# An attention and Fourier kernel on one core: 18 of 64 chunks of scores computed twice instead of 20, in the order of a restated plan

## The chip, the core and the metric

The kernel runs on one core of one Trainium2 chip. The time is the device time of one execution in microseconds; lower is better. A core has five engines that work side by side: TensorE (PE, matmuls; PEld is its loading of weights), VectorE (DVE), ScalarE (ACT), GpSimd (POOL), and SyncE (SP), which here issues every DMA. Each works through its own list of instructions in order and waits on semaphores for the others.

## What is computed

Two independent parts, both in float32, with sequence length S = 2048 and width D = 448. Their results stand side by side in the output (2048 x 896).

```python
# A: Fourier mixing, real part
a = x @ dft_hid_re.T;  b = x @ dft_hid_im.T          # 2048 x 448 each
y = dft_seq_re @ a - dft_seq_im @ b                  # 2048 x 2048 times 2048 x 448, twice
# B: softmax attention, H = 16 heads of Dh = 28
q, k, v = heads(x @ wqkv)
p = softmax(q @ k.T * Dh ** -0.5)                    # 2048 x 2048 for each head
out_b = (p @ v) @ wo
```

## The kernel before

**Products.** Float32 accuracy comes from splitting each operand into a high part (rounded to the fast matmul type fp32r) and a low part (the rest, by a subtraction), and adding three products: high x high, high x low, low x high. ACT rounds a piece (`whi`, L516), POOL subtracts (`wlo`, L522). All of part A, the projections of part B and the output projection are made of such matmuls with 448 or 512 columns: L547 for projections, values and the hidden Fourier step, L662 for the Fourier step along the sequence, L987 for the output projection.

**Attention.** A *unit* is a head h and a chunk c of 512 queries; there are 16 x 4 = 64. For a unit the scores against all 2048 keys are made in 16 matmuls of 128 x 512. The softmax subtracts a maximum first, and there are two ways to get at it:

- `unit_twice`: 16 score matmuls with the queries on the partitions (L754), each followed by a maximum over the row on DVE (L758). The row maxima (`nm`, L762) are turned by a small matmul (L717), split in two parts (L766, L767), written to a scratch tensor in HBM (`nmd`, L773) and read back as two more rows of the operand `q` (L775). Then 16 score matmuls again, now with the keys on the partitions and the maximum already subtracted (L786), and 16 exponentials on ACT straight from PSUM (L790).
- `unit_kept`: 16 score matmuls with the keys on the partitions (L808). ACT copies the scores to SBUF (L415), DVE keeps a running maximum over the 16 tiles (`rm`, L815 and L818). The maximum over partitions is made on DVE with a transpose (L823), reductions (L825, L835), small copies between partitions (L830, L833) and a transpose back (L841); ACT copies it to SBUF (`mb`, L843). Then the maximum is added (negated) to the kept scores, two tiles at a time, on POOL or on DVE (both L858), and ACT takes 8 exponentials over pairs (L862).

For both kinds PE then multiplies by the values, in two groups of 8 matmuls (`pv_group`, L735), and the result is copied out (`ou`). When a head is done, or at the end a chunk of the last two heads, `out_of` adds up four partial sums (L877), fetches the softmax's denominators through a small DMA (`sm`, L882), inverts them, writes them out (`rd`, L884), reads them back spread over partitions (L888), multiplies on POOL (L891) and stores to `ond` (L894). At the very end the output projection reads `ond` (L951, L956), splits it (L969 and L411) and multiplies (L987).

`TWICE` says which chunks of which head are computed twice.

**Order of work.** The order of every engine's list is worked out when the kernel is built. Work is added as tasks with an engine, an assumed duration, a key (when it is due) and what it depends on; `Schedule.run` then plays a clock forward, and whenever an engine is free in that play it takes the ready task with the lowest key and emits its instructions. Keys of units come from two lanes, the twice units and the kept ones, each spread evenly from `T_ATT` to `T_END`; the keys of the Fourier and projection matmuls (`fkey`) run up to `T_FILL`, those of the output projection from `T_OUT`. The assumed durations are constants such as `RAW` (what a DVE instruction adds when it needs the result of the one before), `SMALL` (a small DVE step), `PE_TURN` (PE changes its tile shape), `M448` and `MS` (matmuls). On the chip the engines wait on semaphores, so an assumed duration that is off changes the order and the waits, not the result.

A task ends three times in the play: its engine is free, its result may be used by the same engine ("own"), and its result is seen by the others ("seen"). A DMA's engine is SP, which is free after the issue, long before the data has landed.

Of the kernel before, what the change touches and what calls it, by code (L numbers as in the profile page):

```python
# [14 lines left out]
ALU = mybir.AluOpType  # L15
AX = mybir.AxisListType
# [22 lines left out]
N_WARM = 11  # L39
GV = 8  # L40

TWICE = [(1, 3) if h in (2, 5, 9, 12) else (1,) for h in range(H - 2)] + [(3,), (3,)]
OUT_DVE = True

LAST = (0, 1, 3, 2)
# [8 lines left out]

RAW = 0.16
LANES = 8
FLOW, FLOW_IN = 200.0, 400.0
T_IN = 20.0  # L60
# [1 line left out]
FLOW_AT = 4.1  # L62
X_ROWS = 2.0
AHEAD = 0.15
PE_TURN = 0.22


class Slot:
# [101 lines left out]
class Schedule:  # L170
# [34 lines left out]
    def run(self):  # L205
# [10 lines left out]
        while True:  # L216
            for e in self.ENGINES:
                if not idle[e]:
                    continue
                aside, pick, first = [], None, None  # L220
                if e == "SP" and len(landed) >= LANES and landed[-LANES] > now + 1e-9:
                    heapq.heappush(events, (landed[-LANES], 2, count, "tick", None))
                    continue
                heap = self.ready[e]
                before = now - (AHEAD if e == "PE" else 0.0) + 1e-9
                while heap:
                    item = heapq.heappop(heap)
                    t = item[2]
                    if t.n in done:
                        continue  # L230
                    wants = {}
                    for s in t.use:
                        if s.i is None:
                            wants.setdefault(s.pool, []).append(s)
                    if t.since > before or any(not p.can_take(w, before, now) for p, w in wants.items()) or any(
                            x.lock > now + 1e-9 for x in t.lock):
                        aside.append(item)
                        continue
                    if e == "PE" and mode == 1 and t.mode == 0 and pick is None:
                        if not any(x[2].mode == 1 and x[2].n not in done for x in heap):  # L240
                            pick = t
                            break
                        first = first or item
                        aside.append(item)
                        continue
                    pick = t
                    break
                if pick is None and first:
                    pick = first[2]
                    aside.remove(first)  # L250
                for item in aside:
                    heapq.heappush(heap, item)
                if pick is None:
                    continue
                t = pick
                done.add(t.n)
                for s in t.use:
                    if s.i is None:
                        s.pool.take(s)
                dur = t.engs[e]  # L260
                if e == "PE":
                    if t.mode > mode:
                        dur += PE_TURN
                    mode = t.mode
                lat = t.lat
                if e == "SP":

                    at = now
                    for size, extra in t.dmas:
                        if len(landed) >= LANES:  # L270
                            at = max(at, landed[-LANES])
                        flow = max(flow, at + 0.4) + size / (FLOW if now > T_IN else FLOW_IN)
                        landed.append(max(at + 1.35 + size / 170 + extra, flow + 1.1))
                        at += 0.38
                    dur = at - now
# [14 lines left out]
            while events and events[0][0] <= now + 1e-9:  # L290
# [2 lines left out]
                    idle[x[0]] = True  # L293
                elif what == "own":
                    for n in x[1].then:
                        if x[0] in n.engs and len(n.engs) == 1:
                            n.left -= 1
                            if n.left == 0:
                                self.wake(n)
                elif what == "seen":  # L300
# [3 lines left out]
                        if s.users == 0:  # L304
                            s.home.free.append((s.i, now))
                    for n in t.then:
                        if e in n.engs and len(n.engs) == 1:
                            continue
                        n.left -= 1
                        if n.left == 0:  # L310
                            self.wake(n, now)
# [6 lines left out]
def tile_kernel(ctx, tc, xa, wre, wim, wd, xb, wqkv, wo, out):  # L318
# [67 lines left out]
    eng = {"ACT": nc.scalar, "DVE": nc.vector, "POOL": nc.gpsimd}  # L386


    M512, M448, MS = 0.2335, 0.2065, 0.2365
    ACT_P, ACT_S, DVE_P, POOL_2, SMALL = 0.48, 0.52, 0.60, 1.25, 0.11  # L390

    def pe(key, emit, n=1, d=MS, lat=0.25, **kw):
        return sch.add({"PE": n * d}, key, emit, lat=lat, **kw)
# [8 lines left out]
    def dve(key, emit, d=DVE_P, **kw):  # L402
        return sch.add({"DVE": d}, key, lambda e: emit(), **kw)
# [391 lines left out]
    def unit_kept(u):  # L795
# [6 lines left out]
        for kt in range(NT):  # L802
# [17 lines left out]
        key = t_a + 16 * dt - 20  # L820

        o = bank_s.slot()
        t = dve(key, lambda o=o: nc.vector.transpose(o.t, rm.t), 0.64, deps=[prev], acq=[o], use=[rm])  # L823
        pm = bank_s.slot()
        r = dve(key, lambda o=o: nc.vector.tensor_reduce(  # L825
            pm.t[:, :NT], o.t.rearrange("p (j r) -> p j r", r=32), axis=AX.X, op=ALU.max, negate=True), deps=[t], use=[o, pm], own=RAW)
# [8 lines left out]
        r = dve(key, lambda o=o: nc.vector.tensor_reduce(  # L835
            o.t[:32, :NT], pm.t[:32, :4 * NT].rearrange("p (i j) -> p j i", i=4), axis=AX.X, op=ALU.min), 0.17,
            deps=r, use=[pm, o], own=RAW)
        for n in (32, 64):
            r = dve(key, back(n), SMALL, deps=[r], use=[o], own=RAW)

        t = dve(key, lambda o=o: nc.vector.transpose(pm.t, o.t[:, :NT].unsqueeze(2).to_broadcast([P, NT, 32])), 0.64,  # L841
                deps=[r], use=[pm, o], own=RAW)
        ld = act(key, lambda: nc.scalar.activation(mb.t, pm.t, AF.Copy), deps=[t], use=[pm, mb], lock=[pm])  # L843
        po = bank_s.slot()
        last_pv = None
# [187 lines left out]
```

## Time and profile before

| | |
|---|---|
| median of 3 runs | 1165.56 us (1164.64 to 1166.68) |
| profiled execution, own time | 1163.75 us |
| its span, first to last instruction | 1161.9 us |
| mean granted TensorE clock | 0.999 |
| busy: PE, DVE, ACT, POOL | 1145.3, 1010.8, 1029.1, 884.6 us |
| DMA | 125.19 MB, 35.8% of the 16 DMA engines |

The busy time of an engine is the time in which at least one of its instructions runs. Matmuls follow each other into PE before the one ahead has ended, so the duration of one is longer than what it adds to PE's list; what it adds is seen from start to start. Waits are put down to the instruction that released the waiting one last. A row of the groups reads: line, engine, operation, tiles written <- tiles read, shape, count | busy us, mean ns of one | idle time of the engine just before them, and what ended most of it.

### The profile page before, as it was taken

How to read it: one execution, taken by the hardware profiler on the slowest of the kernel's cores; microseconds unless marked ns; L12 is line 12 of the kernel's file. 1: busy time of each engine (PE TensorE's matmuls, PEld its weight loads, DVE VectorE, ACT ScalarE, POOL GpSimd, SP SyncE). 2: the span in 40 equal slices, each digit the busy share in tenths (PEclk: the TensorE clock that was granted, in tenths of full speed). 3: DMA queues.
4: the chain of work that ended last, by engine and by line, in shares of the span. 5: the costliest groups of instructions: out<-in, count | busy, mean ns of one | idle time of the engine just before them, and what ended most of it. 6: DMA issues, size and time to landing. Idle time of an engine off the chain costs nothing.

```text
span 1161.9 us, 19485 instructions
## 1 busy us (share of the span) xinstructions
PE 1145.3 (99%) x6110; PEld 778.7 (67%) x6110; DVE 1010.8 (87%) x1803; ACT 1029.1 (89%) x1748; POOL 884.6 (76%) x521
## 2 busy tenths in 40 slices
PE   8999999999999999999999999999999999999998
PEld 7876556656676667767666656566666667766677
DVE  6599989999898989999899999998989998799832
ACT  5269999999999899999899999999999999899952
POOL 2138687888789888978888897987989899596630
PEclk9999999999999999999999999999999999999999
DMA  8893344222223222232333232232423223323543
GB/s 259 176 214 120 125 140 148 66 83 73 82 85 102 85 85 82 73 114 78 89 105 100 86 96 65 85 101 90 120 80 96 88 87 114 120 73 92 162 158 109
DMA packets 111880, 125.19 MB, mean 108 GB/s; under 512 B 49368, under 2 KB 63352, under 8 KB 111776
## 3 DMA queue, kind: packets, MB, share of 16 engines
q1 hardware_dynamic: 111776, 123.94, 35.8%
q8 instruction: 48, 0.79, 0.3%
q14 instruction: 56, 0.46, 0.1%
HBM read 90.00 MB, written 33.77 MB: 107 GB/s over the span
## 4 chain that ended last, share of the span: by engine, by line
PE 79%; DVE 9%; ACT 5%; DMA 3%; issue 3%; SPq 0%; DVEq 0%; ACTq 0%
PE bank L662 25%; PE bank L735 17%; PE bank L808 13%; PE bank L547 8%; PE bank L786 6%; PE bank L754 5%; DVE rm L818 4%; PE bank L987 3%; ACT kept L415 2%; DMA kept<-xb 1%; PE bank L877 1%; DVE mx L758 1%; ACT kept L790 1%; ACT kept L862 1%; DVE bank L823 1%
## 5 line engine op out<-in xcount | busy, mean ns | idle before, releaser
L858 POOL TENSOR_TENSOR kept<-kept,mb 128x1024 f32<-128x1024 f32 x254 | 605.7, 2409 | 93.7 <-ACT mb L843 85.6
L818 DVE TENSOR_TENSOR rm<-bank,rm 128x512 f32<-128x512 f32 x616 | 421.7, 685 | 53.7 <-PE bank L808 17.3
L415 ACT ACTIVATE kept<-bank 128x512 f32<-128x512 f32 (+1 forms) x661 | 381.0, 625 | 59.4 <-PE bank L808 34.4
L862 ACT ACTIVATE kept<-kept 128x1024 f32<-128x1024 f32 x341 | 361.2, 1102 | 7.8 <-DVE kept L858 5.0
L662 PE MATMUL bank<-big,whi 128*128 128x448 f32 x1024 | 325.3, 368 | 0.0
L522 POOL TENSOR_TENSOR wlo<-wraw,whi 128x512 fp32r<-128x512 f32 (+1 forms) x166 | 204.2, 1233 | 131.3 <-ACT whi L516 94.8
L808 PE MATMUL bank<-q,k 84*128 84x512 f32 x704 | 277.2, 414 | 2.6 <-DVE bank L841 1.6
L735 PE MATMUL bank<-kept,v 128*32 128x512 f32 x1944 | 240.7, 597 | 1.3 <-DVE mx L758 0.7
L758 DVE TENSOR_REDUCE mx<-bank 128x1 f32<-128x512 f32 x320 | 216.0, 681 | 8.6 <-PE bank L754 7.2
L662 PEld LDWEIGHTS bank<-big,whi 128*128 128x128 f32 x1024 | 193.3, 189 | 32.4 <-issue 5.9
L662 PE MATMUL bank<-big,wlo 128*128 128x448 f32 x512 | 188.4, 368 | 0.2 <-POOL wlo L522 0.2
L808 PEld LDWEIGHTS bank<-q,k 84*128 84x128 f32 x704 | 130.1, 189 | 86.8 <-issue 19.5
L790 ACT ACTIVATE kept<-bank 128x512 f32<-128x512 f32 x290 | 179.3, 637 | 4.1 <-PE bank L786 3.5
L735 PEld LDWEIGHTS bank<-kept,v 128*32 128x32 f32 x1944 | 56.4, 109 | 123.7 <-issue 110.9
L786 PE MATMUL bank<-q,k 86*128 86x512 f32 x320 | 127.4, 408 | 0.7 <-DMA q<-nmd 0.6
L754 PE MATMUL bank<-k,q 84*128 84x512 f32 x320 | 127.3, 407 | 0.3 <-DVE n L767 0.3
L516 ACT ACTIVATE whi<-wraw 128x512 fp32r<-128x512 f32 x167 | 110.8, 667 | 15.3 <-DMA wraw<-wqkv 12.1
L858 DVE TENSOR_TENSOR kept<-kept,bank 128x1024 f32<-128x1024 f32 x87 | 104.1, 1210 | 5.3 <-ACT mb L843 4.9
L662 PEld LDWEIGHTS bank<-big,wlo 128*128 128x128 f32 x512 | 96.9, 189 | 14.5 <-issue 1.0
L547 PE MATMUL bank<-wd,whi 128*128 128x448 f32 x256 | 79.6, 373 | 1.4 <-ACT kept L415 1.1
L786 PEld LDWEIGHTS bank<-q,k 86*128 86x128 f32 x320 | 59.8, 188 | 31.5 <-DVE rm L818 8.1
L754 PEld LDWEIGHTS bank<-k,q 84*128 84x128 f32 x320 | 60.0, 188 | 26.5 <-issue 4.2
(81 smaller groups left out, 1081.1 us busy)
## 6 DMA issues: line engine op xcount, KB each, us to landing
wraw<-wre SPq DMA_DIRECT2D x64, 256.0 KB
wraw<-wim SPq DMA_DIRECT2D x64, 256.0 KB
qkd<-wd SPq DMA_DIRECT2D x32, 256.0 KB
wraw<-xa SPq DMA_DIRECT2D x32, 256.0 KB
k<-qkd SPq DMA_DIRECT2D x64, 112.0 KB
q<-qkd SPq DMA_DIRECT2D x64, 112.0 KB
qkd<-kept SPq DMA_DIRECT2D x24, 256.0 KB
out<-kept SPq DMA_DIRECT2D x27, 224.0 KB
```

Of the source, the lines that this page charges most:

```text
L415: nc.scalar.activation(dst, src, AF.Copy)
L522: b = sch.add(e, at, lambda g: eng[g].tensor_tensor(self.lo.t[:, :n], raw.t[:, :n], f32(self.hi.t)[:, :n], op=ALU.subtract), deps=[a], acq ...
L662: nc.tensor.matmul(o.t[:, :D], a.t[:, k, :], b[:, q * 4 + k, :], start=(q == 0 and k == 0 and j == 0), stop=(q == 3 and k == 3 and j == 2))
L735: nc.tensor.matmul(o.t[j * VW:(j + 1) * VW, :], VT[h].t[:, kt // 4, j, :], pairs[i // 2].t[:, i % 2, :], start=(kt < 4), stop=(kt >= NT - 4))
L754: m = pe(key, lambda e, o=o, kc=kc, qt=qt: nc.tensor.matmul(o.t, q.t[:KR, qt * P:(qt + 1) * P], KT[h][kc].t[:KR, :], start=True, stop=True ...
L758: ms.append(dve(key - 20, lambda o=o, kc=kc, qt=qt: nc.vector.tensor_reduce(mx.t[:, qt, kc:kc + 1], o.t, axis=AX.X, op=ALU.max), deps=[m], ...
L786: m = pe(key, lambda e, o=o, kt=kt: nc.tensor.matmul(o.t, KT[h][kt // 4].t[:KR + 2, kt % 4 * P:(kt % 4 + 1) * P], q.t[:KR + 2, :], start=T ...
L790: es.append(act(key - 20, lambda o=o, p=p: nc.scalar.activation(p.t, o.t, AF.Exp, scale=SCALE), deps=[m], use=[o, p.pair]))
L808: m = pe(key, lambda e, o=o, kt=kt: nc.tensor.matmul(o.t, KT[h][kt // 4].t[:KR, kt % 4 * P:(kt % 4 + 1) * P], q.t[:KR, :], start=True, sto ...
L818: prev = dve(key - 20, lambda o=o: nc.vector.tensor_tensor(rm.t, o.t, rm.t, op=ALU.max), deps=[m, prev], use=[rm, o], lock=[o], own=RAW)
L858: eng[e].tensor_tensor(s.t, s.t, over_pair(pm.t if e == "DVE" else mb.t), op=ALU.add)
L862: es.append(act(key, lambda s=s: nc.scalar.activation(s.t, s.t, AF.Exp, scale=SCALE), 0.96, deps=[sh], use=[s]))
```

## The change

Units: heads 4 and 10 have two chunks computed twice instead of heads 2, 5, 9 and 12; with one of each other head and the last two heads' that makes 18 units twice and 46 kept, before 20 and 44. The rest of the change is in the planner. A task that depends on a DMA no longer counts it as done for SP when the DMA is issued, but when it is seen (the two `"SP"` conditions). Planned landings between 14 and 45 us are 1.5 us later. Assumed durations change: `RAW`, a new `RAW_S` for the transpose and reduction after the running maximum, `SMALL`, one reduction of 0.17 to 0.25, `PE_TURN`, `M448`; the small steps no longer get `RAW` on top. The due times `T_END`, `T_FILL` and `T_OUT` are later.

```diff
-TWICE = [(1, 3) if h in (2, 5, 9, 12) else (1,) for h in range(H - 2)] + [(3,), (3,)]
+TWICE = [(1, 3) if h in (4, 10) else (1,) for h in range(H - 2)] + [(3,), (3,)]
...
-RAW = 0.16
+RAW = 0.19
+RAW_S = 0.12
...
-PE_TURN = 0.22
+PE_TURN = 0.33
...
-                        landed.append(max(at + 1.35 + size / 170 + extra, flow + 1.1))
+                        landed.append(max(at + 1.35 + size / 170 + extra + (1.5 if T_IN - 6 < now < 45 else 0.0), flow + 1.1))
...
-                        if x[0] in n.engs and len(n.engs) == 1:
+                        if x[0] in n.engs and len(n.engs) == 1 and x[0] != "SP":
...
-                        if e in n.engs and len(n.engs) == 1:
+                        if e in n.engs and len(n.engs) == 1 and e != "SP":
...
-    M512, M448, MS = 0.2335, 0.2065, 0.2365
-    ACT_P, ACT_S, DVE_P, POOL_2, SMALL = 0.48, 0.52, 0.60, 1.25, 0.11
+    M512, M448, MS = 0.2335, 0.2050, 0.2365
+    ACT_P, ACT_S, DVE_P, POOL_2, SMALL = 0.48, 0.52, 0.60, 1.25, 0.21
...
-    T_ATT, T_END, T_FILL, T_OUT = 34.0, 1085.0, 1120.0, 1085.0
+    T_ATT, T_END, T_FILL, T_OUT = 34.0, 1100.0, 1130.0, 1100.0
...
-        t = dve(key, lambda o=o: nc.vector.transpose(o.t, rm.t), 0.64, deps=[prev], acq=[o], use=[rm])
+        t = dve(key, lambda o=o: nc.vector.transpose(o.t, rm.t), 0.64, deps=[prev], acq=[o], use=[rm], own=RAW_S)
...
-        r = [dve(key, beside(i), SMALL, deps=[r], use=[pm], own=RAW) for i in (1, 2, 3)]
+        r = [dve(key, beside(i), SMALL, deps=[r], use=[pm]) for i in (1, 2, 3)]
```

More of the change, by code (lines that the diff above doesn't have):

```diff
@@ L822, in unit_kept @@
         o = bank_s.slot()
-        t = dve(key, lambda o=o: nc.vector.transpose(o.t, rm.t), 0.64, deps=[prev], acq=[o], use=[rm])
+        t = dve(key, lambda o=o: nc.vector.transpose(o.t, rm.t), 0.64, deps=[prev], acq=[o], use=[rm], own=RAW_S)
         pm = bank_s.slot()
         r = dve(key, lambda o=o: nc.vector.tensor_reduce(
-            pm.t[:, :NT], o.t.rearrange("p (j r) -> p j r", r=32), axis=AX.X, op=ALU.max, negate=True), deps=[t], use=[o, pm], own=RAW)
+            pm.t[:, :NT], o.t.rearrange("p (j r) -> p j r", r=32), axis=AX.X, op=ALU.max, negate=True), deps=[t], use=[o, pm], own=RAW_S)
         def beside(i):
@@ L833, in back @@
             return lambda: nc.vector.tensor_copy(o.t[n:2 * n, :NT], o.t[:n, :NT])
-        r = [dve(key, beside(i), SMALL, deps=[r], use=[pm], own=RAW) for i in (1, 2, 3)]
+        r = [dve(key, beside(i), SMALL, deps=[r], use=[pm]) for i in (1, 2, 3)]
         r = dve(key, lambda o=o: nc.vector.tensor_reduce(
-            o.t[:32, :NT], pm.t[:32, :4 * NT].rearrange("p (i j) -> p j i", i=4), axis=AX.X, op=ALU.min), 0.17,
-            deps=r, use=[pm, o], own=RAW)
+            o.t[:32, :NT], pm.t[:32, :4 * NT].rearrange("p (i j) -> p j i", i=4), axis=AX.X, op=ALU.min), 0.25,
+            deps=r, use=[pm, o])
         for n in (32, 64):
-            r = dve(key, back(n), SMALL, deps=[r], use=[o], own=RAW)
+            r = dve(key, back(n), SMALL, deps=[r], use=[o])
         t = dve(key, lambda o=o: nc.vector.transpose(pm.t, o.t[:, :NT].unsqueeze(2).to_broadcast([P, NT, 32])), 0.64,
-                deps=[r], use=[pm, o], own=RAW)
+                deps=[r], use=[pm, o])
         ld = act(key, lambda: nc.scalar.activation(mb.t, pm.t, AF.Copy), deps=[t], use=[pm, mb], lock=[pm])
```

## The prediction

> **What bounds the kernel now.** I read the page first, then the table of stretches, the timeline of TensorE, the groups, the waits and the tail. The page's share of busy time:
>
> ```profile
> span 1161.9 us, 19485 instructions
> ## 1 busy us (share of the span) xinstructions
> PE 1145.3 (99%) x6110; PEld 778.7 (67%) x6110; DVE 1010.8 (87%) x1803; ACT 1029.1 (89%) x1748; POOL 884.6 (76%) x521
> ```
>
> The chain that ended last, by engine:
>
> ```profile
> PE 79%; DVE 9%; ACT 5%; DMA 3%; issue 3%; SPq 0%; DVEq 0%; ACTq 0%
> ```
>
> TensorE (PE) is idle for 1161.9 - 1145.3 = 16.6 us and carries most of the chain. The table of stretches says where (columns: stretch, length, busy time of PE, PEld, DVE, ACT, POOL, then granted clock and DMA share):
>
> ```profile
> 100.00:1085.00 985.00, 977.54 (x5302) 647.76 (x5301) 903.52 (x1580) 934.71 (x1584) 831.21 (x472) 1.00 0.31 95
> 0.00:100.00 100.00, 94.55 (x430) 74.12 (x431) 73.75 (x162) 54.04 (x91) 30.66 (x36) 1.00 0.81 206
> ```
>
> From 100 to 1085 us, where attention and the Fourier work run side by side, PE idles 985.00 - 977.54 = 7.5 us. ACT idles there 985.00 - 934.71 = 50.3 us, DVE 81.5 and POOL 153.8. So the kernel is as long as PE's list of matmuls, and ACT is the second bound, 5% behind. What a change takes off PE's list comes off the end, if the other engines can carry what they get for it.
>
> **What the change takes from PE.** A chunk computed twice has 32 score matmuls (16 for the maximum, L754, 16 for the exponentials, L786); a chunk kept has 16 (L808). Two chunks go from twice to kept, so 32 matmuls go, and two of the small transposes of L717. Price of one, from starts and not from durations, since matmuls overlap:
>
> ```profile
> 854.27 0.86 PE L754 MATMUL bank<-k,q 84*128 84x512 f32 x3
> 854.97 0.37 PE L662 MATMUL bank<-big,whi 128*128 128x448 f32 x1
> ```
>
> Three score matmuls took 854.97 - 854.27 = 0.70 us, 0.233 each. 32 of them are 7.5 us. The transpose:
>
> ```profile
> 286.42 0.27 PE L717 MATMUL bank<-ident,nm 128*4 128x128 f32 x1 [0.50 <-DVE nm L762]
> 286.52 0.47 PE L754 MATMUL bank<-k,q 84*128 84x512 f32 x1
> 287.91 0.50 PE L808 MATMUL bank<-q,k 84*128 84x512 f32 x1 [0.92 <-DVE bank L841]
> ```
>
> 286.52 - 286.42 = 0.10 us, two are 0.2. PE's list gets 7.7 us shorter. The second product (L735) is the same for both kinds of chunk, so nothing comes back to PE.
>
> **What it puts on the other engines.** Their groups on the page, with 44 kept and 20 twice chunks now:
>
> ```profile
> L858 POOL TENSOR_TENSOR kept<-kept,mb 128x1024 f32<-128x1024 f32 x254 | 605.7, 2409 | 93.7 <-ACT mb L843 85.6
> L818 DVE TENSOR_TENSOR rm<-bank,rm 128x512 f32<-128x512 f32 x616 | 421.7, 685 | 53.7 <-PE bank L808 17.3
> L415 ACT ACTIVATE kept<-bank 128x512 f32<-128x512 f32 (+1 forms) x661 | 381.0, 625 | 59.4 <-PE bank L808 34.4
> L862 ACT ACTIVATE kept<-kept 128x1024 f32<-128x1024 f32 x341 | 361.2, 1102 | 7.8 <-DVE kept L858 5.0
> ...
> L758 DVE TENSOR_REDUCE mx<-bank 128x1 f32<-128x512 f32 x320 | 216.0, 681 | 8.6 <-PE bank L754 7.2
> ...
> L790 ACT ACTIVATE kept<-bank 128x512 f32<-128x512 f32 x290 | 179.3, 637 | 4.1 <-PE bank L786 3.5
> ...
> L858 DVE TENSOR_TENSOR kept<-kept,bank 128x1024 f32<-128x1024 f32 x87 | 104.1, 1210 | 5.3 <-ACT mb L843 4.9
> ```
>
> ACT: a kept chunk has 661/44 = 15 copies of 0.625 (9.4 us) and 8 exponentials over pairs of 1.102 (8.8), 18.2 us; a twice chunk has 16 exponentials of 0.637, 10.2 us. That is +8.0 us a chunk, +16 us for two. POOL: 254/44 = 5.8 shifts of 2.409, +13.9 us a chunk, +28 us. For DVE the reshuffling of the maximum comes on top, from the groups by shape:
>
> ```profile
> L841 DVE STREAM_TRANSPOSE bank<-bank 128x512 f32<-128x512 f32 x44 | 32.2, 731 | 1.4
> L823 DVE STREAM_TRANSPOSE bank<-rm 128x512 f32<-128x512 f32 x44 | 31.7, 720 | 1.1 <-ACT kept L415 0.3
> L825 DVE TENSOR_REDUCE bank<-bank 128x16 f32<-128x512 f32 x44 | 30.7, 699 | 3.2 <-ACT kept L790 0.8
> ```
>
> Kept: 14 maxima of 0.685 (the fifteenth, L815, is of the same size and taken at the same), 0.73 + 0.72 + 0.70, and 87/44 = 2 shifts of 1.21: 14.8 us; twice: 16 of 0.681, 10.9. So +4 us a chunk, +8 us, and about a microsecond each for the small copies between.
>
> I price this at nothing, and the cover is the idle time in the long stretch: 16 of ACT's 50.3 us, 10 of DVE's 81.5, 28 of POOL's 153.8. If that cover is gone, ACT is first: the stretch shrinks by 7.7 us, so ACT's share goes from 934.7/985 = 95% to 950.7/977.3 = 97%. This is the thin place of the forecast, and a rival below. What ACT now waits for in that stretch, from its waits:
>
> ```profile
> ACT kept L415 <- PE bank L808: 9.4, 23, 1.0
> ```
>
> A good part of ACT's idle time is waiting for score matmuls, that is for PE; those gaps close by themselves when PE has less to do. It speaks for the cover holding.
>
> **What the new plan does.** All the other edits change costs and keys in the planner that writes the order of instructions; no instruction gets cheaper by them. (a) A DMA that needs another DMA's data: the old plan puts it right behind, and the queue of SP stands still until the first has landed.
>
> ```profile
> SPq L888 <- DMA rd<-sm: 25.4, 18, 3.7
> SPq L775 <- DMA nmd<-n: 25.2, 21, 2.0
> ```
>
> 50.6 us of standing queue. Behind it are loads of score operands (L689, L707) and of Fourier weights (L515). Yet who waits for these DMAs is small on PE and sizable only on POOL:
>
> ```profile
> PE bank L786 <- DMA q<-nmd: 0.6, 1, 0.6
> ```
>
> ```profile
> POOL kept L891 <- DMA kept<-rd: 15.1, 9, 5.6
> ```
>
> The new plan sends other loads first and the second DMA when its data is there. POOL is not the bound and PE's part is 0.6 us, so I take -0.6 us for it; its ends are 0 and, were all of POOL's 15.1 us passed on, -15.1, which I dismiss since POOL has 153.8 us idle beside it. (b) The 1.5 us added to landings planned between 14 and 45 us: bounded by the idle 100 - 94.55 = 5.5 us of the first stretch, which includes the unavoidable start; either sign, taken at 0, ends -2.5 and +2.5 (half of it). (c) Costs of small DVE steps, of a switch of PE between tile shapes, and keys: attention's last due time moves 15 us back (1085 to 1100), the Fourier work's 10 us (1120 to 1130), so attention sits 5 us later against it. The effect is another order of the same matmuls. Its gain is bounded by the 7.5 us that PE idles from 100 to 1085; a loss of the same size is the nearest bound on the other side. Taken at 0.
>
> **The tail.** It has to give way too. The last second product, the last loads of attention's result, the last output matmuls, from timelines of PE, SP, POOL and ACT:
>
> ```profile
> 1113.75 1.92 PE L735 MATMUL bank<-kept,v 128*32 128x512 f32 x16
> ...
> 1149.22 9.15 PE L987 MATMUL bank<-wd,k 128*128 128x448 f32 x44
> ```
>
> ```profile
> 1128.89 0.77 SPq L888 DMA_DIRECT2D kept<-rd  x2
> ...
> 1134.86 1.09 SPq L956 DMA_DIRECT2D kept<-ond  x2
> ```
>
> ```profile
> 1131.50 1.28 POOL L891 TENSOR_TENSOR kept<-kept 64x512 f32<-64x512 f32 x1 [5.62 <-DMA kept<-rd]
> ```
>
> ```profile
> 1146.56 0.42 ACT L969 ACTIVATE k<-kept 128x256 fp32r<-128x256 f32 x1 [1.30 <-PE bank L987]
> 1147.17 1.03 ACT L969 ACTIVATE k<-kept 128x256 fp32r<-128x256 f32 x3 [0.20 <-PE bank L987]
> ```
>
> A DMA lands about 1131.50 - (1128.89 + 0.77) = 1.8 us after its issue, so the last loads (1134.86 + 1.09 = 1135.95) were there by 1137.8. The splits that feed the last matmuls need 1149.22 - 1146.56 = 2.7 us, so those matmuls could have begun at 1140.5, 8.7 us before they did: the tail is filled with PE work, and it holds 8.7 us of slack. My 8.3 us fit in even if attention ends where it ends now (1115.7).
>
> Sum: -7.5 - 0.2 - 0.6 = -8.3 us. The profiled execution took 1163.75 (its span and 1.85 us around it): 1155.4, a span of about 1153.6. The median of the runs, 1165.56, lies 1.8 us above that execution; there the sum gives 1157.3.
>
> **Rivals.** *The new order closes PE's gaps too* (faster still): all of the 7.5 us between 100 and 1085 goes, 1149.8. For it: PE's named waits stand behind DVE steps (the rows at 286 us) whose costs the new plan states anew. Against it: 7.5 us over 985 is little left to win.
>
> *The gain is eaten* (no change): PE's waits behind the longer DVE lists double, +7.5 us, 1164.8.
>
> *ACT becomes the bound* (slower). If ACT's gaps don't close and its 16 us push attention's end from 1115.7 to 1131.7, the rest of the tail still needs 1161.9 - 8.7 - 1115.7 = 37.5 us: a span of 1169.2, 1172.9 on the median's scale. It decides from the point at which attention ends more than 8.7 us later; below that, the tail's slack swallows it. For it: 97% of busy time on ACT, attention's keys 5 us later against the Fourier work. Against: busy time overlaps itself on ACT, and a good part of its gaps are PE's doing.
>
> *The clock falls more often* (slower). Where DVE made PE wait at 286 us, the granted clock sank for a few microseconds (clock is the column before the last two):
>
> ```profile
> 285.00:290.00 5.00, 3.58 (x15) 2.17 (x12) 4.57 (x11) 4.27 (x7) 2.65 (x2) 0.87 0.42 143
> 290.00:295.00 5.00, 5.00 (x24) 3.73 (x27) 4.06 (x7) 4.33 (x9) 5.00 (x3) 0.79 0.01 3
> ```
>
> That is 5 x 0.13 + 5 x 0.21 = 1.7 us lost beside 0.50 + 0.92 = 1.4 us of waiting. If the added 7.5 us of waits came in five such clusters, 5 x 1.7 = 8.5 us would come on top: 1173.3. The Trainium skill ("TensorE: Matmul & The Clock Gate", "What's actually happening") says that the PE clock is halved after an idle window of about 3.4 us. By that rule single waits as short as these would not lower it; the rows show a fall beside two waits of 1.4 us together, so the trace is harsher than the rule here. By the rule this rival falls away and the sum stays 1157.3. Against it: one such place between 100 and 1085 us.
>
> **How the numbers follow.** Forecast 0.50, its own range 1153 to 1162; still faster 0.16; no change 0.08; ACT the bound 0.19; clock 0.07. Predicted: 1157.3. Low end: all gaps closed and the start 2.5 us better, 1147. High end: the slower rivals' 1173. Outside remain about 0.05 below and 0.1 above. A measurement of this kernel tells about 0.2% (2.3 us) from no change. Faster 0.66, same 0.08, slower 0.26.
>
> **What would show it.** Right: 288 matmuls on each of L754 and L786 and 736 on L808; PE still busy 99% of a span near 1154, its busy time some 8 us less; ACT up 16, POOL 28, DVE 8 to 10 us; the waits of L775 and L888 on other DMAs gone from SP's queue with PE hardly touched; the last output matmuls start before 1143. Wrong: the last second product later than 1124 and gaps in PE behind it (ACT), or PE idle in the long stretch well over 7.5 us and more stretches with a clock under 1 (the other two), or the 32 matmuls gone and PE's busy time not smaller.

## The result: no difference, and the profile after

The changed kernel takes 1164.86 us (median of 22 runs, 1159.41 to 1167.96), the kernel before 1164.57 (22 runs, 1160.42 to 1167.37): a ratio of 1.0001, 95% interval 0.999 to 1.0013. The forecast was 1157.3 and "faster".

The page of the changed kernel, whose lines are numbered one higher from L58 on (the score matmuls are L755, L787 and L809 now). Its profiled execution took 1165.2 us.

```profile
span 1163.4 us, 19480 instructions
## 1 busy us (share of the span) xinstructions
PE 1142.1 (98%) x6076; PEld 775.1 (67%) x6076; DVE 1012.8 (87%) x1800; ACT 1044.8 (90%) x1782; POOL 917.5 (79%) x534
```

PE has 34 matmuls less, ACT 15.7 us more and POOL 32.9 us more, as the change says. DVE has only 2.0 us more, not 8 to 10; one reason is that of the 16 shifts that two kept units bring, 14 went to POOL (263 before, 277 after) and 2 to DVE. But PE's busy time is only 3.2 us shorter, not 8, and its idle time rose from 16.6 to 21.3 us. The table of stretches (stretch, length, busy time of PE, PEld, DVE, ACT, POOL, granted clock, DMA share, GB/s), over the long stretch and the tail, and the tail of the kernel before:

```profile
100.00:1085.00 985.00, 978.28 (x5306) 646.41 (x5305) 903.09 (x1584) 957.73 (x1629) 865.66 (x486) 1.00 0.31 96
...
1085.00:1162.00 77.00, 70.45 (x350) 54.67 (x348) 37.11 (x59) 33.52 (x67) 16.33 (x11) 0.98 0.43 139
```

```profile
1085.00:1162.00 77.00, 73.22 (x381) 56.87 (x379) 33.50 (x62) 40.35 (x77) 22.69 (x15) 1.00 0.46 148
```

In the long stretch ACT's share went from 95% to 97% as worked out, and PE got through 5306 records of matmuls where it got through 5302 before. The tail lost: PE idles 6.6 of its 77 us, before 3.8. The last output matmuls start at 1145.87 us and not before 1143; the last second product ends at 1118.9, so the forecast's sign of ACT as the bound (later than 1124) isn't there. The planner's rule for DMAs did what it says, though not to the end. SP's own waits in these two lines, of one DMA on another, fell from 50.6 to 18.3 us:

```profile
SPq L776 <- DMA nmd<-n: 9.4, 9, 1.8
...
SPq L889 <- DMA rd<-sm: 8.9, 6, 2.4
```

The tail holds the largest single stall of PE. Timeline of PE around it (start, duration, what, idle time before and its releaser):

```profile
1093.20 1.91 PE L736 MATMUL bank<-kept,v 128*32 128x512 f32 x12
1099.18 2.40 PE L736 MATMUL bank<-kept,v 128*32 128x512 f32 x4 [4.08 <-ACT kept L791]
```

PE stands in the middle of a second product for 4.08 us. The engine named is ACT, but ACT had itself stood still, longer:

```profile
1097.59 1.06 ACT L863 ACTIVATE kept<-kept 128x1024 f32<-128x1024 f32 x1 [6.88 <-DVE kept L859]
1098.55 1.06 ACT L791 ACTIVATE kept<-bank 128x512 f32<-128x512 f32 x2
```

And DVE, which released ACT, was not idle but inside two instructions. The timeline of all engines in that window:

```profile
1088.85 7.57 DVE L412 TENSOR_TENSOR k<-kept,k 128x256 fp32r<-128x256 f32 x2
...
1090.01 1.48 POOL L892 TENSOR_TENSOR kept<-kept 64x512 f32<-64x512 f32 x1
...
1091.44 4.70 POOL L859 TENSOR_TENSOR kept<-kept,mb 128x1024 f32<-128x1024 f32 x2
...
1096.35 1.21 DVE L859 TENSOR_TENSOR kept<-kept,bank 128x1024 f32<-128x1024 f32 x1
```

Two subtractions for the output projection (their median in this trace is 0.42 us each) took 7.57 us, and the second ended 0.3 us after POOL's two shifts had. The Trainium skill ("SBUF — State Buffer", "Who interferes with whom" and "Summary: rules for kernel authors") has a rule for this: a DVE instruction with two inputs in SBUF contends with a GpSimd instruction that reads SBUF, and whichever comes second is blocked until the other has finished. L412 reads two SBUF tiles, POOL's shifts too, and the trace agrees, though the second subtraction was held for longer than one POOL instruction. Such meetings are older than the change: in the kernel before four of these subtractions (L411) took 0.77 to 1.60 us beside POOL, and none made PE stand so long. The DVE shift at 1096.35 was queued behind, ACT's exponential of it behind that, then the exponentials that PE had waited for (L791), and PE's product at the end. The clock then fell for a spell:

```profile
1075.00:1100.00 25.00, 20.92 (x113) 13.62 (x113) 20.75 (x26) 17.71 (x32) 14.31 (x10) 0.98 0.39 121
1100.00:1125.00 25.00, 25.00 (x124) 16.83 (x121) 10.06 (x17) 15.22 (x28) 6.38 (x5) 0.95 0.60 181
```

25 x 0.02 + 25 x 0.05 = 1.7 us. With the 4.1 us of standing that is 5.8 us: enough to eat most of a gain of 8.3, but only if that gain was there. The experiments ask both.

### The profile page after: what moved, and what is told of

It is laid out like the page before. It is cut to its first block, busy times and chain, and to the rows that moved or that the text cites. A ratio compares the mean times of both kernels' runs of the same rounds, so it can differ in the third digit from the quotient of the medians.

```text
span 1163.4 us, 19480 instructions
## 1 busy us (share of the span) xinstructions
PE 1142.1 (98%) x6076; PEld 775.1 (67%) x6076; DVE 1012.8 (87%) x1800; ACT 1044.8 (90%) x1782; POOL 917.5 (79%) x534
## 4 chain that ended last, share of the span: by engine, by line
PE 84%; DVE 6%; ACT 4%; issue 2%; DMA 2%; POOL 1%; SPq 1%; DVEq 0%; ACTq 0%; POOLq 0%
PE bank L663 27%; PE bank L736 18%; PE bank L809 14%; PE bank L548 9%; PE bank L787 6%; PE bank L755 5%; PE bank L988 3%; DVE rm L819 2%; ACT kept L416 2%; PE bank L878 1%; POOL kept L859 1%; ACT kept L863 1%; DVE k L412 1%; DMA kept<-wqkv 1%; DVE mx L759 1%
## 5 line engine op out<-in xcount | busy, mean ns | idle before, releaser
L859 POOL TENSOR_TENSOR kept<-kept,mb 128x1024 f32<-128x1024 f32 x269 | 641.1, 2405 | 88.4 <-ACT mb L844 85.6
L819 DVE TENSOR_TENSOR rm<-bank,rm 128x512 f32<-128x512 f32 x644 | 441.1, 685 | 53.4 <-ACT kept L416 20.0
L416 ACT ACTIVATE kept<-bank 128x512 f32<-128x512 f32 (+1 forms) x696 | 410.7, 658 | 59.7 <-PE bank L809 34.6
L863 ACT ACTIVATE kept<-kept 128x1024 f32<-128x1024 f32 x354 | 385.1, 1133 | 12.8 <-DVE kept L859 8.7
L809 PE MATMUL bank<-q,k 84*128 84x512 f32 x736 | 286.4, 414 | 4.5 <-ACT kept L416 2.7
L759 DVE TENSOR_REDUCE mx<-bank 128x1 f32<-128x512 f32 x288 | 194.8, 680 | 12.1 <-PE bank L755 11.0
L809 PEld LDWEIGHTS bank<-q,k 84*128 84x128 f32 x736 | 134.9, 189 | 99.5 <-DVE rm L819 15.3
L791 ACT ACTIVATE kept<-bank 128x512 f32<-128x512 f32 x262 | 169.3, 669 | 5.3 <-PE bank L787 5.1
L755 PE MATMUL bank<-k,q 84*128 84x512 f32 x288 | 117.8, 412 | 2.2 <-DMA q<-qkd 1.8
L787 PE MATMUL bank<-q,k 86*128 86x512 f32 x288 | 115.8, 409 | 0.7 <-DMA q<-nmd 0.4
L755 PEld LDWEIGHTS bank<-k,q 84*128 84x128 f32 x288 | 54.2, 189 | 31.1 <-issue 6.0
L548 PE MATMUL bank<-big,whi 128*128 128x512 f32 x196 | 70.1, 402 | 3.4 <-DVE big L412 1.3
```

The lines of the kernel that those rows point to most:

```text
L416: nc.scalar.activation(dst, src, AF.Copy)
L548: nc.tensor.matmul(o.t[:, :cols], w(), x(), start=(i == 0), stop=(i == n - 1))
L755: m = pe(key, lambda e, o=o, kc=kc, qt=qt: nc.tensor.matmul(o.t, q.t[:KR, qt * P:(qt + 1) * P], KT[h][kc].t[:KR, :], start=True, stop=True ...
L759: ms.append(dve(key - 20, lambda o=o, kc=kc, qt=qt: nc.vector.tensor_reduce(mx.t[:, qt, kc:kc + 1], o.t, axis=AX.X, op=ALU.max), deps=[m], ...
L787: m = pe(key, lambda e, o=o, kt=kt: nc.tensor.matmul(o.t, KT[h][kt // 4].t[:KR + 2, kt % 4 * P:(kt % 4 + 1) * P], q.t[:KR + 2, :], start=T ...
L809: m = pe(key, lambda e, o=o, kt=kt: nc.tensor.matmul(o.t, KT[h][kt // 4].t[:KR, kt % 4 * P:(kt % 4 + 1) * P], q.t[:KR, :], start=True, sto ...
```

## The experiments

Theory A at the start: PE's list sets the time; the change takes 7.7 us off it, pays 3.0 back in changes of tile shape (109 before, 118 after, counted in the order of PE's instructions; about 0.33 us each) and loses the rest in the tail's stall. Rival B: ACT has become the bound. Rival C: nothing but scatter from one order to another. Times are medians; ratios are to the kernel before in the same session, with the 95% interval. Differences between two kernels are differences of their ratios times 1164.5 us; by the intervals of the two they are uncertain by about 3 us. Where a sentence says how much of a time is the clock, that is an estimate: one minus the granted clock on record for a run, times its span, averaged over the kernel's runs.

### The parts of the change, and the tail's stall

**The units alone** (`b_tw18`): the kernel before with

```diff
-TWICE = [(1, 3) if h in (2, 5, 9, 12) ...
+TWICE = [(1, 3) if h in (4, 10) ...
```

> The kernel before with the units of the change alone (18 twice, heads 4 and 10), planner and due times as before. Theory A (PE's list, minus what the order gives back): 32 score matmuls and 2 transposes less are -7.7 us; the products with the values are merged less often, 118 changes of tile shape instead of 109 at about 0.33 us each, +3.0; so -4.7 us against before (ratio 0.996), and more if no collision of DVE and POOL falls into its tail. Rival B (ACT has become the bound, the units' gain is lost on it): 0 to +8 us, attention ends later. Rival C (nothing but scatter from one order to another): anything within 3 us of before.

Measured: 1177.98 us, ratio 1.0112 (1.0089 to 1.0134), 13 us slower. Theory A in its simple form is out: on the old plan two units less make the kernel slower. A part of it is the clock: the profiled execution, 16.5 us longer than that of before, has five spells of 3.41 us at half speed against one, 6.8 us more; over all runs it is some 4 of the 13 us. What the rest is stays open.

**The plan alone** (`a_tw20`): the changed kernel with heads 2, 5, 9 and 12 again.

> The changed kernel with the old 20 twice units (heads 2, 5, 9, 12): the new plan alone. Theory A: against the changed kernel +7.7 us of PE work and 7 changes of tile shape less (111), -2.3; so some 5 us over the changed kernel, unless the stall of its tail (PE idle 4.1 us, half clock 3.4 us after it) is gone here, then about the same. Rival B: faster than the changed kernel, since ACT has 16 us less to do.

Measured: 1166.16 us, ratio 1.0015 (0.9999 to 1.0031). The tail's stall is here too, 5.3 us this time and at the sum of the partial results, which waits for a DVE copy queued behind the subtractions. So it comes with the plan and not with the units. PE's wait, its DVE and its POOL:

```profile
PE bank L878 <- DVE ou L418: 5.3, 1, 5.3
```

```profile
1097.37 7.70 DVE L412 TENSOR_TENSOR k<-kept,k 128x256 fp32r<-128x256 f32 x4
```

```profile
1097.04 4.93 POOL L859 TENSOR_TENSOR kept<-kept,mb 128x1024 f32<-128x1024 f32 x2
1101.93 2.85 POOL L523 TENSOR_TENSOR wlo<-wraw,whi 128x512 fp32r<-128x512 f32 x2
```

Four subtractions in 7.70 us, the last ending 0.3 us after POOL's last at 1104.78. Here each got in after one POOL instruction (2.61 us at most); why one was held through three in the changed kernel isn't explained.

**The collision taken away** (`a_outpool`): the subtractions go to POOL, which works through its list in order and so can't collide with itself.

```diff
-OUT_DVE = True
+OUT_DVE = False
```

> The changed kernel with the subtraction of the output projection's operand split (L412) on POOL instead of DVE, so that it cannot collide with POOL. Theory A (in the tail two of these DVE instructions took 7.57 us instead of 0.8 beside POOL's shifts, DVE's last shifts came late, PE idled 4.08 us and the clock halved for 3.4 us): the stall goes, -4 to -6 us against the changed kernel, ratio to before 0.995 to 0.997. Rival B (ACT is late there anyway): no change, PE still idles some 4 us before the last product of that unit. Rival D (POOL is now late with its own shifts): +2 us or more.

Measured: 1158.02 us, ratio 0.9948 (0.993 to 0.9966): 6.2 us less than the changed kernel, and faster than both kernels. Up to 1088 us the two traces have the same instructions in the same order on every engine; from 1050 to 1100 us the changed kernel falls 8.0 us behind. The stall is gone; the DVE shifts of that unit now run beside POOL's work:

```profile
1090.13 8.01 DVE L859 TENSOR_TENSOR kept<-kept,bank 128x1024 f32<-128x1024 f32 x7 [0.67 <-ACT mb L844]
```

```profile
1091.21 1.29 POOL L892 TENSOR_TENSOR kept<-kept 64x512 f32<-64x512 f32 x1
1092.47 2.40 POOL L859 TENSOR_TENSOR kept<-kept,mb 128x1024 f32<-128x1024 f32 x1
```

Seven shifts in 8.01 us, 1.14 each: a DVE instruction of the same kind with one input in PSUM isn't held up beside the same POOL instructions. That is the rule's other half.

**Its control** (`b_outpool`): the same edit of the kernel before.

> The kernel before with the output projection's split on POOL, the control to the same edit of the changed kernel (which took 6.8 us off it). Theory A (the stall is of the changed kernel's tail: there POOL's long shifts and DVE's splits fall together for 7 us; in the kernel before the splits between 1094 and 1107 us were drawn out to 1.6 us at most): -2 to 0 us against before. Rival E (the edit is good for any order and says nothing of the change): -5 us or more.

Measured: 1164.60 us, ratio 1.0001 (0.9984 to 1.0018). The edit is worth nothing there, so it was the collision in the changed kernel's tail that it removed.

**The landings** (`a_noland`): the changed kernel without the 1.5 us between 14 and 45 us.

```diff
-... + size / 170 + extra + (1.5 if T_IN - 6 < now < 45 else 0.0), flow + 1.1))
+... + size / 170 + extra, flow + 1.1))
```

> The changed kernel without the 1.5 us added to planned landings between 14 and 45 us. Theory A (the first 50 us lost 1.1 us of PE's busy time against before, partly by POOL subtractions that now fall beside DVE's at 23 to 27 us): -1 to -2 us against the changed kernel. Otherwise no change.

Measured: 1165.46 us, ratio 1.0008 (0.9989 to 1.0027): no difference from the changed kernel. The loss of 1.1 us in the first 50 us isn't explained by it; traces of one and the same order differ there by more (2.9 to 5.0 us between `a_tw20_op` and three kernels below that share its order up to there).

**The units again, without the stall** (`a_tw20_op`): `a_outpool` with the old 20 units.

> The changed kernel with the split on POOL and with the old 20 twice units. Set beside a_outpool (18, 1158.0 us) it prices the two units without the tail's stall. Theory A: +7.7 us of PE work, 7 changes of tile shape less (-2.3): 1163 us. Rival B (ACT takes back what PE gains): 1158 or less.

Measured: 1158.09 us, ratio 0.9946 (0.9925 to 0.9967), the same as with 18. So the two units, the part of the change from which the forecast took 7.7 us, are worth nothing in this pair of orders, within some 3 us; the plan without its stall is worth 6.3 us at 20 units.

**The parts of the plan**, each set back by itself in `a_outpool`:

- the rule for DMAs (`a_sp_op`): the two `"SP"` conditions out again.

> The changed kernel with the split on POOL and with the old rule for a DMA that needs another's data (sent right behind it). Theory A (it stands in SP's queue, hardly anything on PE waits for it): within 2 us of a_outpool. Rival F (the order of DMAs is what makes 18 units possible): 5 us or more above a_outpool.

Measured: 1174.04 us, ratio 1.009 (1.0068 to 1.0112): 16.5 us slower, some 6 of them the clock.

- the assumed costs (`a_cost_op`): `RAW`, `RAW_S`, `PE_TURN`, `M448`, `SMALL` and the steps after the running maximum as before.

> The changed kernel with the split on POOL and with the old assumed costs (RAW, the small DVE steps, the change of tile shape, M448), the rule for DMAs, the landings and the due times being the new ones. The units alone on the old plan took 13.5 us more than before, so something in the plan is worth about 18 us to 18 units. If it is the costs (theory G): 8 us or more above a_outpool, with PE waiting for DVE. If not: within 3 us of a_outpool.

Measured: 1170.26 us, ratio 1.0051 (1.0032 to 1.007): 12 us slower, some 3 of them the clock.

- the due times (`a_Tb_op`): `T_END`, `T_FILL`, `T_OUT` as before.

> The changed kernel with the split on POOL and the old due times (1085, 1120, 1085): attention's keys 5 us earlier against the Fourier work. If the later due times are what makes 18 units fit: 4 us or more above a_outpool (1158.0). If not: within 2 us.

Measured: 1161.26 us, ratio 0.9981 (0.9967 to 0.9995): 3.8 us slower, little more than the uncertainty.

- the rule for DMAs at 20 units (`a_tw20_sp_op`).

> The changed kernel with the split on POOL, the old 20 units and the old rule for a DMA that needs another's data. At 18 units the old rule took 16 us more. Theory J (a standing queue of SP starves PE of Fourier pieces whatever the units): 8 us or more above a_tw20_op (1158.1). Rival K (it matters only where ACT, DVE and POOL have no slack left): within 4 us of a_tw20_op.

Measured: 1170.33 us, ratio 1.0057 (1.0035 to 1.0079), 13 us over `a_tw20_op`. The rule is worth 13 to 16 us at both numbers of units, within the new plan. These prices don't add up to the 6.3 us of the whole: with the old costs, due times and landings the old rule took 1164.5, with the new ones 1170. The parts of a plan are worth what they are worth only beside each other. The rule alone on the kernel before was not tried.

How the old rule costs that much is not shown. The longest gap in SP's issues in `a_sp_op` looks like an answer and is none. Its SP there, and SP's wait (us in total, times, longest):

```profile
527.78 0.36 SPq L516 DMA_DIRECT2D wraw<-wre  x1
539.89 0.33 SPq L678 DMA_DIRECT2D yd<-kept  x1
542.61 0.33 SPq L516 DMA_DIRECT2D wraw<-wre  x1
```

```profile
SPq L678 <- DVE kept L677: 24.1, 6, 11.7
```

SP issues nothing for 12 us, because it stands before a store until DVE has made a copy: not for another DMA. Nor does this starve PE. Pieces of the Fourier matrices go through three buffers (`wraw`), and the next load, at 542.61, was waiting for POOL to free one of them. Three pieces lay loaded; the one issued at 522.53 us was rounded by ACT only 16 us later, and POOL, with four shifts ahead in its list, came to it after that:

```profile
538.37 0.64 ACT L517 ACTIVATE whi<-wraw 128x512 fp32r<-128x512 f32 x1
```

```profile
531.85 9.50 POOL L859 TENSOR_TENSOR kept<-kept,mb 128x1024 f32<-128x1024 f32 x4 [4.47 <-ACT mb L844]
541.28 1.30 POOL L523 TENSOR_TENSOR wlo<-wraw,whi 128x512 fp32r<-128x512 f32 x1
```

From 537.5 to 543.1 us PE is left with score matmuls, which go at the pace at which ACT and DVE free PSUM banks. Its timeline and its stretches:

```profile
529.06 0.73 PE L809 MATMUL bank<-q,k 84*128 84x512 f32 x2
538.78 1.10 PE L809 MATMUL bank<-q,k 84*128 84x512 f32 x2
541.31 0.79 PE L787 MATMUL bank<-q,k 86*128 86x512 f32 x1 [0.29 <-DVE rm L819]
```

```profile
520.00:530.00 10.00, 10.00 (x62) 6.18 (x55) 7.48 (x16) 7.72 (x14) 7.38 (x5) 1.00 0.39 111
530.00:540.00 10.00, 9.62 (x41) 7.32 (x40) 9.52 (x14) 10.00 (x19) 8.15 (x4) 1.00 0.02 5
540.00:550.00 10.00, 9.67 (x35) 5.96 (x39) 8.56 (x15) 8.88 (x14) 8.55 (x5) 0.66 0.24 84
```

Two score matmuls take 0.73 us at 529.06 and 1.10 at 538.78, the clock being full at both: waits of PE show as longer matmuls. So PE is "busy" for 9.67 of 10 us although it waits, and no wait of PE here names a DMA. The clock falls at 541.3 us (0.66 over the stretch), which also lowers the number of records there.

### The number of units, and scatter

**16 units** (`a_tw16_op`, one chunk of each head) and **19** (`a_tw19_op`), both in `a_outpool`:

```diff
-... (4, 10) else (1,) ...      # 18
+... () else (1,) ...           # a_tw16_op
+... (3, 7, 11) else (1,) ...   # a_tw19_op
```

> The changed kernel with the split on POOL and only 16 units twice (one chunk of each head). 20 and 18 units both took 1158 us. Theory A as it stands now (two units take 7.7 us off PE's list, and the longer lists of ACT, DVE and POOL give it back as waits and changes of tile shape, 121 here): no gain left, 1158 to 1164. Rival H (PE's list sets the time and 18 units with heads 4 and 10 are only an unlucky order): 1152 or less.

Measured: 1168.40 us, ratio 1.0046 (1.0029 to 1.0063).

> The changed kernel with the split on POOL and 19 units twice (two chunks of heads 3, 7 and 11), 106 changes of tile shape instead of 118. Theory A: half the units' PE work of a_outpool comes back (+3.8), 12 changes less (-4.0), fewer waits: 1155 to 1158. Rival C (scatter between orders of several us): anything from 1153 to 1163.

Measured: 1163.14 us, ratio 1.0000 (0.9986 to 1.0014). So 20, 19, 18, 16 units take 1158, 1163, 1158, 1168 us. The 19 have fewest changes of tile shape (106) and are 6 us slower than both neighbours: rival C is real, and a gain of 7.7 us from two units could drown in it. Much of this scatter is the clock: it takes about 5, 10, 3 and 8 us of these four, and what is left (1152.9, 1153.5, 1155.3, 1160.6 us) rises as units are taken away. Each number of units was tried in one order only.

### One engine's work at a time, in a fixed order

All of these kernels changed the order as well. The next five keep the order of every engine and change one engine's work alone, so that the same PE instruction can be set side by side in two traces.

**PE less** (`a_less_op` from `a_outpool`, `b_less` from before):

```diff
-                        nc.tensor.matmul(o.t[:, :D], a.t[:, k, :], b[:, q * 4 + k, :], ...
+                        out_ or nc.tensor.matmul(o.t[:, :D], a.t[:, k, :], b[:, q * 4 + k, :], ...
...
+  out_ = j == 2 and k == 1 and (q == 1 or (q == 2 and tt % 5 == 0))
```

> a_outpool (18 units, split on POOL, 1158.0 us) with the same order on every engine, but 40 matmuls of the Fourier step (L663, low times high, one or two for each of 32 row blocks) left out; that part of the result is then less accurate. Theory A (PE's list sets the time): 40 x 0.205 = 8.2 us less, 1150. Rival B (another engine sets it): 1156 to 1158.

Measured: 1156.25 us, ratio 0.9921 (0.99 to 0.9943), 3.1 us less than `a_outpool`. The edit leaves out 64 matmuls and not 40: it reads `tt` only when the plan is played, and then `tt` is 15 for every row block, so that two go from each of the 32. Their groups in `a_outpool` and in `a_less_op`:

```profile
L663 PE MATMUL bank<-big,wlo 128*128 128x448 f32 x512 | 188.1, 367 | 0.0
```

```profile
L663 PE MATMUL bank<-big,wlo 128*128 128x448 f32 x448 | 164.7, 368 | 0.0
```

> The kernel before with the same order on every engine, the same 40 matmuls of the Fourier step left out. Theory A: 8.2 us less than before (ratio 0.993). Rival B: within 2 us of before.

Measured: 1162.35 us, ratio 0.9971 (0.9955 to 0.9986), 3.4 us less than before. At 0.205 us from start to start, 64 matmuls are 13.1 us, and they give 3.1 us (uncertain by 3.3) and 3.4 (by 1.8): a microsecond of PE is worth about a quarter. PE's busy time fell by 5.0 us (1141.2 to 1136.2) and 3.5 (1145.3 to 1141.8): most of what was left out comes back as longer matmuls. These are Fourier matmuls; score matmuls were not left out in a fixed order.

**ACT more** (`a_act_op`, from `a_tw20_op`):

```diff
-ld = act(key, lambda: nc.scalar.activation(mb.t, pm.t, AF.Copy), ...
+ld = act(key, lambda: [nc.scalar.activation(mb.t, pm.t, AF.Copy) for _ in range(1 if c == 0 else 2)], ...
```

> a_tw20_op (20 units, split on POOL, 1158.1 us) with the same order on every engine, but the copy of the shift on ACT (L844) made twice in 28 kept units, 28 x 0.48 = 13 us more of ACT and nothing else. Theory B2 (ACT's idle time does not cover what two units bring): 5 us or more above 1158. Theory A2 (it covers it): within 2 us.

Measured: 1172.26 us, ratio 1.0053 (1.0032 to 1.0073): 12.5 us more for 13 us of ACT. The long stretch and the last second products of `a_tw20_op`, then of `a_act_op`:

```profile
100.00:1085.00 985.00, 981.30 (x5346) 652.09 (x5339) 890.99 (x1563) 942.28 (x1611) 843.77 (x477) 1.00 0.32 95
```

```profile
100.00:1085.00 985.00, 978.14 (x5277) 639.52 (x5279) 881.65 (x1548) 942.88 (x1615) 837.95 (x472) 1.00 0.31 94
```

```profile
L736 PE MATMUL bank<-kept,v x144: 592/592/617, 1050.0 to 1109.6; 128*32 128x512 f32 x144
```

```profile
L736 PE MATMUL bank<-kept,v x176: 592/592/617, 1050.2 to 1126.1; 128*32 128x512 f32 x176
```

Attention ends 16.5 us later (1126.1 instead of 1109.6), nearly as the forecast's rival had it: the same PE instruction comes 2.9 us later at 100 us, which is scatter of the start, and 16.5 us later at 1100, so 13.6 us grew bit by bit in between. PE's busy time in the stretch differs by 3.2 us, but it holds 69 records of matmuls less, and PEld, the loading of weights, is 12.6 us less busy: PE was waiting while "busy". ACT's busy time is the same, though it had more to do. A reservation: the second copy also holds back the shifts that wait for it (POOL's waits for `mb` in this stretch grow from 53.6 to 70.2 us), so this is the price of ACT work at that place, which need not be that of ACT work elsewhere.

**POOL more** (`a_pool_op`, from `a_tw20_op`): `times` is 2 for every seventh piece.

```diff
-            b = sch.add(e, at, lambda g: eng[g].tensor_tensor(
+            b = sch.add(e, at, lambda g: [eng[g].tensor_tensor(
...
-                ... op=ALU.subtract),
+                ... op=ALU.subtract) for _ in range(times)],
```

> a_tw20_op with the same order on every engine, but every seventh subtraction of a Fourier piece on POOL (L523) made twice, some 23 x 1.25 = 28 us more of POOL and nothing else, as much as two more kept units bring. Theory B3 (POOL's idle time does not cover it): 5 us or more above 1158. Otherwise within 2 us.

Measured: 1166.91 us, ratio 1.0017 (1.0001 to 1.0032): 8.3 us more for 28 us of POOL, an engine that idles 141 us of that stretch. Here too it grows bit by bit: the same PE instruction comes 4.9 us later at 100 us and 13.7 us at 1100. And here too the work stands where another engine, PE, waits for what follows it.

**ACT less** (`a_actless_op`, from `a_tw20_op`):

```diff
-nc.scalar.activation(s.t, s.t, AF.Exp, scale=SCALE), 0.96
+nc.scalar.activation(s.t[:, :n], s.t[:, :n], AF.Exp, scale=SCALE), 0.96      # n = 1 if i == 0 and c else 2
```

> a_tw20_op (20 units, split on POOL, 1158.1 us) with the same order on every engine, but in 28 kept units the first of the 8 exponentials takes one tile instead of two, 28 x 0.47 = 13 us less of ACT; those halves of the probabilities are left unexponentiated. Theory L (ACT's list sets the time): 8 us less or more, 1150. Theory M (PE and ACT are both close behind each other in this order, so more of either costs and less of one alone gains little): 1 to 5 us less.

Measured: 1158.38 us, ratio 0.9942 (0.9926 to 0.9957): no difference, and the same PE instruction comes 4.3 us later at 100 us and 4.4 at 1100: nothing was won anywhere. So ACT does not set the time either. More of it cost nearly its full length, less of it, at another place, brought nothing.

**ACT's work moved to DVE** (`a_cp_op`): `a_outpool` with three copies of scores in a kept unit free to go to either, planned anew, so in another order.

```diff
-{"ACT": ACT_P, "DVE": DVE_P} if kt == 1 else {"ACT": ACT_P}
+{"ACT": ACT_P, "DVE": DVE_P} if kt in (1, 5, 9) else {"ACT": ACT_P}
```

> The changed kernel with 18 units, the split on POOL, and three copies of scores of a kept unit (tiles 1, 5, 9 instead of 1 alone) free to go to ACT or DVE in the plan; it puts 68 of them on DVE instead of 22, 46 x 0.48 = 22 us less of ACT and 46 x 0.60 = 28 us more of DVE. Changes of tile shape 113 instead of 118. Theory L: faster than a_outpool (1158.0) by 5 us or more. Rival C (scatter of orders, DVE now full): 1158 or more.

Measured: 1179.06 us, ratio 1.0117 (1.0097 to 1.0136), 20 us slower, some 8 of them the clock. How much of the rest is the load on DVE and how much the new order isn't known.

## Why the prediction was wrong, point by point

**"What a change takes off PE's list comes off the end."** This step failed first. In a fixed order 13.1 us of matmuls less gave 3.1 and 3.4 us. The mistake was to read 7.5 us of idle time as all that PE waits for. A matmul that waits for its PSUM bank is drawn out in the profile (in `a_sp_op` two took 1.10 us at 538.78 us and 0.73 at 529.06), so waits hide in the busy time; the records that PE gets through in a stretch show them, and the sum of busy time does not. The Trainium skill ("Trainium Kernel Development and Optimization", "Performance Expectations") calls matmul busy time a bad metric for how close a kernel is to roofline, "because matmuls are pipelined"; the trace agrees that it hides waits, with 69 matmul records fewer in the same stretch at 3.2 us less of busy time.

**"I price this at nothing, and the cover is the idle time."** The load was right on ACT (+15.7 us) and nearly on POOL (+32.9 instead of 28) and too high on DVE (+2.0 instead of 8 to 10); the price was wrong. In a fixed order 13 us more of ACT cost 12.5 us and 28 us more of POOL 8.3, although the idle time of the stretch was several times that for POOL. The forecast's doubt, "the thin place of the forecast", was the right place; the rival built on it, ACT as the one bound, was wrong too: 13 us less of ACT gave nothing. A reading that fits these runs, and that they don't prove, is that the written order sets the time: each engine waits in line for another one's result at a planned moment, so that later costs (tried on ACT and POOL) and earlier brings little (tried on PE and ACT). With the plan made anew, two units come out at 0 (1158.02 against 1158.09): PE's shorter list and the longer lists of the others leave nothing over, and which of them takes how much is open.

**(a) The rule for DMAs, taken at -0.6 us.** Mis-sized by a factor of 20 and more: 16.5 us at 18 units and 13 at 20, within the new plan. The step had the right queue and the right number (50.6 us of standing, now 18.3), but looked for the price among the waits of PE that name a DMA, and it isn't there. Some 6 of the 16.5 us are the clock; by which way the rest reaches PE stays open, and as the order changes with the rule, a part may be the order's.

**(c) Costs and keys, taken at 0 within 7.5 us.** The costs were worth 12 us at 18 units, some 3 of them the clock, outside these ends; the due times 3.8.

**(b) The landings**, taken at 0: right (`a_noland`, 0.8 us from the changed kernel).

**The tail, "8.7 us of slack".** The slack was counted in one engine's time, and the new order put a collision there that the step did not look for: 4.1 us of standing and 1.7 us of clock in the trace, 6.2 us by the runs with and without it, 8.0 at 20 units. Of the two slower rivals, "the clock falls more often" named a part of it. The first trace had hints: L858 on DVE and POOL and L411 on DVE share those microseconds of the tail, and L411 takes up to 1.60 us there.

Together: the plan -6.3 us, its collision +6.2, the units 0, each uncertain by 2 to 3 us. The measured 0 is two effects of the plan against each other, neither of which was in the sum, and what the forecast did sum came to nothing.

## What to carry to other kernels

In a kernel whose engines are kept in step by a written order, an idle share is not a cover: price added work by adding it in a fixed order, and a saving by leaving it out, before re-planning; and count in the trace that the edit took out what it was meant to. Judge PE by matmuls done in a stretch, not by busy time, and follow a wait two engines back: here PE named ACT, ACT named DVE, and DVE was held up by POOL. When the parts of a change are priced, set each back by itself; here a result of zero hid a gain and a loss of 6 us each, and moving one flag kept the gain (1158.0 us).

## What the runs showed of the hardware

A DVE instruction with two SBUF inputs can be held up by a run of POOL instructions, not just by one: it sat for 6.16 us (the longest of L412 in the changed kernel, and again in `a_noland`) through one multiplication and two shifts that followed each other without a gap. In `a_tw20` and in the kernel before it got in between two of them, after 2.61 us at most. The granted clock falls in spells of 3.41 us, or twice that, to one half, and a spell needs no PE that shows as idle for long: in `a_sp_op` it fell at 541.3 us, and PE was idle for only 0.7 of the 3.4 us before, in short gaps among matmuls that waited. By the Trainium skill ("TensorE: Matmul & The Clock Gate", "What's actually happening") the clock halves after an idle window of about 3.4 us; the length of a spell agrees, and so does the fall behind the 4.08 us of standing in the changed kernel's tail, but at 541.3 us an idle window as such wasn't there. Executions of one and the same kernel differ by such spells in part: the changed kernel's run from 1159.4 us at a mean clock of 0.999 to 1168.0 at 0.996, and 0.003 of 1166 us are 3.5 of these 8.6 us.
